# Attention feeding a two-layer MLP: transposing the first units on TensorE, attending them a step sooner, and summing half of the first large chunk's first layer ahead, pair by pair

## The chip, the cores and the metric

One NeuronCore of a Trainium2 chip runs the whole kernel as one launch. The engines are TensorE (PE; its weight loads are listed as PEld), VectorE (DVE), ScalarE (ACT), GpSimd (POOL) and SyncE (SP), which issues the DMAs here. Each engine works through its own list of instructions in order and waits at semaphores for the others. The metric is the device time of one execution in microseconds (us), given as the median of several runs.

## The reference

Eight batches of eight heads with 576 tokens and head width 64. Each row of scores keeps its 32 largest entries before the softmax; the heads' outputs are put side by side as 512 features of 4608 tokens, and a two-layer MLP with a leaky ReLU follows.

```python
scores = scale * np.matmul(q, k.transpose(0, 1, 3, 2))
kth = np.partition(scores, -top_k, axis=-1)[..., -top_k:-top_k + 1]   # top_k = 32
scores = np.where(scores >= kth, scores, -1000000000.0)
scores = scores - np.max(scores, axis=-1, keepdims=True)
attn = np.exp(scores)
attn = attn / (np.sum(attn, axis=-1, keepdims=True) + 1e-09)
attn_out = np.matmul(attn, v)
...
x = attn_out.transpose(0, 2, 1, 3).reshape(B * S, H * D)   # 4608 x 512
h = x @ w_in                                               # 512 x 2048
g = np.maximum(0.01 * h, h)
return g @ w_out                                           # 2048 x 512
```

## The kernel before

**Units.** The attention is cut into 144 units. A whole unit is 128 queries of one pair of heads, and works on 128 x 2 x 576 scores. As 576 is four and a half times 128, the last (or, in odd batches, first) 64 queries of two pairs share a unit. A batch has 18 units: in even batches four query tiles, each over the four pairs (whole), and then two shared ones. So units 0 to 3 are the first 128 queries of batch 0 for pairs 0 to 3, units 4 to 7 the next 128, and so on up to 15; units 16 and 17 are the shared ones.

**Steps.** A loop over s writes the order of every engine's list by hand (the scheduler is told to leave it alone). At step s VectorE picks the 32 largest of unit s (`top_k`, L250 to L258, in four rounds, `slot()`); POOL masks unit s-1 (L268, L269), ScalarE takes its exponents (L272) and their sum (`ze`, L277); and unit s-2 is divided by that sum: reciprocal on VectorE (`rz`, L281), two multiplications on ScalarE (L284), together `weights_of`. Then unit s-2 is transposed. In the usual way (`transpose`) ScalarE splits the words into halves (two copies, L293), SyncE writes them to memory (L294) and reads them back by a DMA transpose (L298) into `wT`, of which there are three buffers. For the units in `HASTY` TensorE transposes instead (nine instructions, L308, into the PSUM buffers called `wide`), and ScalarE copies the result to `wT` (`keep_transposed`, L314).

Where `weights_of` stands in a step depends on the unit: usually after the first round of picks; in steps below `HURRY` (20) after the second (`late`), unless s-1 or s-2 is in `HURRIED`; and before the first round if s-2 is in `HURRIED` (`at_first`, again below step 20). In a list worked in order, an earlier place of the reciprocal also makes VectorE wait earlier for the sum.

**Values.** Two units at a time are multiplied with v on TensorE (L335, into a `wide` buffer) and copied by ScalarE (L349) into `x`, the MLP's input. `values_at` says at which step this stands, and whether in its middle or at its end: for units below 14, four steps after the pair, MIDDLE; after that three steps, END; and one step less for the pairs in `HURRIED` (15, 23, 31).

**Scores.** At the end of each even step the scores of units s+2 and s+3 are computed (L220): each unit takes a `wide` buffer (two of them, two banks each), and both share the one `narrow` buffer (two banks). ScalarE copies them out (L227). Units 0 and 1 go through `first_scores` instead (L236), which takes two `wide` buffers a unit and no `narrow`.

**MLP.** The tokens are cut into chunks, two of 128 and then 17 of 256. A chunk may start when all of its units have their values (`ready_at`, `attended`): chunk 0 after units 0 to 3, chunk 1 after 4 to 7, chunk 2 after 8 to 15. `mlp(ch)` is a generator. For the small chunks (`EARLY`) the first layer is `hidden_of_few` (L359), with Prelu on ScalarE (L364), transposes (L375) and their copies (L376). For the large ones it is 64 matmuls (L391), four (one for each pair's 128 features, `c`) for each of 16 blocks `f` of the hidden width; two blocks share a PSUM bank `ph`, and ScalarE's Prelu reads both (L397) into `gT`. The second layer is 16 matmuls for each 128 tokens (L403, bank `pz`), a copy to `o_sb` (L412) and the store (L413). `ph`, `pt` and `pz` share a pool of two banks.

Seven times a step `mlp_steps(budget)` lets the generator issue some matmuls: until chunk 2 is ready 500 columns' worth, then the backlog spread evenly to the step at which the next chunk is ready. So the place of every matmul in TensorE's list is fixed when the program is built.

Of the kernel before, what the change touches and what calls it, by code (L numbers as in the profile page):

```python
# [9 lines left out]
F32 = mybir.dt.float32  # L10
# [10 lines left out]
def kernel(  # L21
# [13 lines left out]
    nc = tc.nc  # L35
    NPAIR, P, S = qT.shape
# [8 lines left out]
    HP = DMODEL // P  # L45
    B = NPAIR // HP
    HS = S // 2
    NARROW = 224
    WIDE = S - NARROW
    NFC = DFF // P  # L50
    WCH = 1024
    LEFT = S % P
    assert D == 64 and S == 576 and HP == 4 and B % 2 == 0 and LEFT == 64
    CHUNKS = [128] * 2 + [256] * 17
    assert sum(CHUNKS) == B * S
    CHMAX = max(CHUNKS)
# [23 lines left out]
    w_in = [const.tile([P, DFF], F32, name=f"w_in{c}") for c in range(HP)]  # L80
# [113 lines left out]
    units = []  # L194
    for b in range(B):
        first = b % 2 == 1
        whole = [Unit(b, [b * HP + hp], q0 + LEFT * first)
                 for q0 in range(0, S - LEFT, P) for hp in range(HP)]
        left = [Unit(b, [b * HP + hp, b * HP + hp + 1], 0 if first else S - LEFT)
                for hp in range(0, HP, 2)]  # L200
        units += left + whole if first else whole + left

    def scores(us):


        narrow = ps_sc.tile([P, 2, 512], F32, name="narrow")
        ps = {}
        for k, u in enumerate(us):
            wide = ps_sc.tile([P, 2, 512], F32, name="wide", bufs=2)
            ps[u] = ((wide[:, :, 0:WIDE], 0, WIDE),  # L210
                     (narrow[:, :, k * NARROW:(k + 1) * NARROW], WIDE, S))

        order = ((us[0], 0), (us[0], 1), (us[1], 1), (us[1], 0))
        for u, part in order:
            to, k0, k1 = ps[u][part]
            for n in range(0, len(u.parts), 2):
                for i, pi, side, r0 in u.parts[n:n + 2]:
                    qt, kt = qk_of[pi]
                    d = slice(side * D, (side + 1) * D)
                    nc.tensor.matmul(to[r0:r0 + u.rows, i, :], qt[d, u.q0:u.q0 + u.rows],  # L220
                                     kt[d, k0:k1], start=True, stop=True)
        for u in us:
            u.both = work.tile([P, 2, S], F32, name="s_sb", bufs=5)
            u.s = [u.both[:, i, :] for i in range(2)]
        for u, part in order:
            to, k0, k1 = ps[u][part]
            nc.scalar.copy(u.both[:, :, k0:k1], to)  # L227

    def first_scores(u):

        ps = [ps_sc.tile([P, 2, 512], F32, name="wide", bufs=2) for i in range(2)]
        for half in range(2):
            for i, pi, side, r0 in u.parts:
                qt, kt = qk_of[pi]
                d = slice(side * D, (side + 1) * D)
                nc.tensor.matmul(ps[i][:, half, 0:HS], qt[d, u.q0:u.q0 + P],  # L236
                                 kt[d, half * HS:(half + 1) * HS], start=True, stop=True)
        u.both = work.tile([P, 2, S], F32, name="s_sb", bufs=5)
        u.s = [u.both[:, i, :] for i in range(2)]
        for i in range(2):  # L240
            nc.scalar.copy(u.s[i].rearrange("p (h n) -> p h n", h=2), ps[i][:, :, 0:HS])
# [76 lines left out]
    x_of = {}  # L318
# [53 lines left out]
    def turned(j, g_of):  # L372
# [3 lines left out]
        nc.scalar.copy(gT[:, 4 * j:4 * (j + 1), 0:P], pt)  # L376
        yield 2 * P

    def mlp(ch):

        n = CHUNKS[ch]
        t0 = sum(CHUNKS[:ch])
        x = x_of[ch]
        if ch < EARLY:
            yield from hidden_of_few(ch, x)
        for f0 in range(0, NFC if ch >= EARLY else 0, 2):
            ph = ps_ml.tile([P, 2, CHMAX], F32, name="ph", tag="ml")
            for i in range(2):
                f = f0 + i
                for c in range(HP):  # L390
                    nc.tensor.matmul(  # L391
                        ph[:, i, 0:n], w_in[c][:, f * P:(f + 1) * P], x[c][:, 0:n],
                        start=(c == 0), stop=(c == HP - 1),
                    )
                    if c == 1 or i == 0 and c == HP - 1:
                        yield 2 * max(n, 225)
            nc.scalar.activation(gT[:, f0:f0 + 2, 0:n], ph[:, :, 0:n], AF.Prelu, alpha=SLOPE)  # L397
            yield 2 * max(n, 225)
        for r0 in range(0, n, P):
            m = min(P, n - r0)  # L400
            pz = ps_ml.tile([P, 512], F32, name="pz", tag="ml")
            for f in range(NFC):
                nc.tensor.matmul(  # L403
                    pz[0:m, 0:DMODEL], gT[:, f, r0:r0 + m], w_out[f // 4][:, f % 4, :],
                    start=(f == 0), stop=(f == NFC - 1),
                )
                if f % 2 and f + 1 < NFC:
                    yield 2 * DMODEL
                if f == 7 and ch in few:
                    yield from turned(NFC // 4 - 1, few[ch])  # L410
            o_sb = work.tile([P, DMODEL], F32, name="o_sb", bufs=1)
            nc.scalar.copy(o_sb[0:m], pz[0:m, 0:DMODEL])  # L412
            nc.sync.dma_start(out[t0 + r0:t0 + r0 + m, :], o_sb[0:m])  # L413
            yield 2 * DMODEL

    def mlp_cost(ch):
        n = CHUNKS[ch]
        if ch < EARLY:
            return NFC * DMODEL + NFC // 4 * (HP * 512 + 2 * P)
        return NFC * HP * max(n, 225) + -(-n // P) * NFC * DMODEL  # L420
# [4 lines left out]
    def mlp_steps(budget):  # L425
        owed[0] += budget
        while owed[0] > 0:
            if running[0] is None:
                if not ready:
                    owed[0] = 0.0  # L430
                    return
                running[0] = mlp(ready.pop(0))
            cost = next(running[0], None)
            if cost is None:
                running[0] = None
            else:
                owed[0] -= cost
                backlog[0] -= cost
# [2 lines left out]

    LAG = 3
    HURRY = 20
    HURRIED = (15, 23, 31)
    HASTY = (14, 15, 23, 31)
    UNHURRIED = 14
    MIDDLE, END = 0, 1

    def values_at(n):

        if n < UNHURRIED:
            return (n | 1) + LAG + 1, MIDDLE
        return (n | 1) + LAG - ((n | 1) in HURRIED), END

    steps = units

# [11 lines left out]
    def attended(*place):  # L468
        for at, ch in ready_at:
            if at == place:  # L470
                ready.append(ch)
                backlog[0] += mlp_cost(ch)

    def slot_budget(s):

# [9 lines left out]
    with tc.manual_schedule():  # L485
# [52 lines left out]
        for s in range(len(steps) + LAG + 1):  # L538
            cur, old, older, new = unit(s), unit(s - 1), unit(s - 2), ()
            if s % 2 == 0:  # L540
                new = [u for u in steps[s + 2:s + 4] if u]
            picks = top_k(cur) if cur else iter(())
            budget = slot_budget(s)

            def slot():
                next(picks, None)

            at_first = s < HURRY and s - 2 in HURRIED
            if at_first:
                weights_of(older)  # L550
            slot()
            if old:
                mask(old, 0)
                mask(old, 1)
            late = s < HURRY and not {s - 1, s - 2} & set(HURRIED)
            if older and not late and not at_first:
                weights_of(older)
            mlp_steps(budget)
            weighed = values(s, MIDDLE)
            at_once = s - 2 in HURRIED or any(at == (s, MIDDLE) for at, _ in ready_at)  # L560
            if at_once:
                keep(weighed, s, MIDDLE)
            slot()
            if older and late:
                weights_of(older)
            if s - 2 in HASTY:
                transpose_in_haste(older)
            mlp_steps(budget)
            if old:
                exponents(old, 0)  # L570
            mlp_steps(budget)
            if older:
                keep_transposed(older) if s - 2 in HASTY else transpose(older, lambda: mlp_steps(budget))
            if not older or s - 2 in HASTY:
                mlp_steps(budget)
            slot()
            slot()
            mlp_steps(budget)
            if old:
                exponents(old, 1)  # L580
                sums(old)
            mlp_steps(budget)
            if not at_once:
                keep(weighed, s, MIDDLE)
            if new and s < HURRY:
                scores(new)
            keep(values(s, END), s, END)
            if new and s >= HURRY:
                scores(new)
            budget = slot_budget(s + 1)  # L590
            mlp_steps(budget)
            load_more(s)
# [59 lines left out]
```

## Time and profile before

| what | value |
|---|---|
| median of 8 runs | 1472.07 us (1469.79 to 1473.73) |
| profiled execution | 1473.73 us, its span 1471.8 us |
| TensorE busy | 1394.5 us (95%), mean granted clock 0.981 |
| VectorE busy | 1322.1 us (90%) |
| ScalarE, POOL busy | 1097.9 us (75%), 1096.4 us (74%) |
| first-layer matmuls of chunk 0 start | 134.03 us |
| values of units 14 and 15 end, chunk 2 starts | 228.7 us |
| VectorE's period from step 16 on | 207.72, 216.80, 225.56, 234.36 us |

A busy share is an average over stages: the first 64 us load and round the weights, from 66 us on the steps run, and after about 1385 us only the MLP of the last chunks is left. Times in the trace are counted from the start of the span. An f32 matmul of 256 or 512 columns appears as two records (x32 is 16 matmuls); a transpose of 128 columns as one. In a row of the timeline, the number in brackets is the engine's idle time before it, and the arrow names what ended it.

### The profile page before, as it was taken

How to read it: one execution, taken by the hardware profiler on the slowest of the kernel's cores; microseconds unless marked ns; L12 is line 12 of the kernel's file. 1: busy time of each engine (PE TensorE's matmuls, PEld its weight loads, DVE VectorE, ACT ScalarE, POOL GpSimd, SP SyncE). 2: the span in 40 equal slices, each digit the busy share in tenths (PEclk: the TensorE clock that was granted, in tenths of full speed). 3: DMA queues.
4: the chain of work that ended last, by engine and by line, in shares of the span. 5: the costliest groups of instructions: out<-in, count | busy, mean ns of one | idle time of the engine just before them, and what ended most of it. 6: DMA issues, size and time to landing. Idle time of an engine off the chain costs nothing.

```text
span 1471.8 us, 24096 instructions
## 1 busy us (share of the span) xinstructions
PE 1394.5 (95%) x8068; PEld 927.8 (63%) x8068; DVE 1322.1 (90%) x3400; ACT 1097.9 (75%) x1979; POOL 1096.4 (74%) x743
## 2 busy tenths in 40 slices
PE   6716999999999999999999999999999999999999
PEld 2304548676766666767666666666666666666674
DVE  7899999999999999999999999999999999999600
ACT  8657878777887777777777777777777777777710
POOL 3188888878788888888888787878787878787700
PEclk9957999999999999999999999999999999999999
DMA  9724543655367455665557544765467544654510
GB/s 332 298 67 135 145 113 100 178 152 149 92 185 203 137 137 154 167 180 145 145 158 191 151 137 122 186 186 150 123 165 208 137 136 131 169 135 138 143 50 14
DMA packets 388795, 222.29 MB, mean 151 GB/s; under 512 B 333888, under 2 KB 333888, under 8 KB 386624
## 3 DMA queue, kind: packets, MB, share of 16 engines
q1 hardware_dynamic: 388672, 220.77, 53.8%
q8 instruction: 63, 1.03, 0.3%
q14 instruction: 60, 0.49, 0.1%
HBM read 46.14 MB, written 92.01 MB: 94 GB/s over the span
## 4 chain that ended last, share of the span: by engine, by line
PE 80%; DVE 13%; DMA 3%; ACT 2%; issue 1%; SPq 0%; DVEq 0%; ACTq 0%
PE pz L403 31%; PE ph L391 30%; PE wide L335 10%; DVE tops L255 6%; PE wide L220 6%; DVE pairs L258 4%; PE narrow L220 3%; DMA raw<-in_weights_dram 2%; DVE pairs L250 1%; DMA wT<-apart 1%; ACT wT L127 0%; DVE w_out L155 0%; DMA apart<-split 0%; ACT split L293 0%; PE wide L308 0%
## 5 line engine op out<-in xcount | busy, mean ns | idle before, releaser
L268 POOL TENSOR_SCALAR pen<-s_sb,tops 128x576 f32<-128x576 f32 x288 | 637.5, 2213 | 210.6 <-DVE tops L255 142.7
L255 DVE MAX8 tops<-pairs 128x8 f32<-128x288 f32 (+1 forms) x1152 | 635.9, 591 | 0.0
L403 PE MATMUL pz<-w_out,gT 128*128 128x512 f32 x1152 | 505.3, 595 | 2.4 <-ACT scale L364 2.4
L391 PE MATMUL ph<-x,w_in 128*128 128x256 f32 x2176 | 482.6, 381 | 0.0
L258 DVE MATCH_REPLACE8 pairs<-tops,pairs 128x288 f32<-128x288 f32 (+1 forms) x864 | 460.1, 538 | 0.0
L391 PEld LDWEIGHTS ph<-x,w_in 128*128 128x128 f32 x2176 | 409.5, 190 | 76.4 <-issue 22.2
L269 POOL TENSOR_TENSOR s_sb<-s_sb,pen 128x576 f32<-128x576 f32 x288 | 406.6, 1412 | 24.1
L403 PEld LDWEIGHTS pz<-w_out,gT 128*128 128x128 f32 x1152 | 216.4, 190 | 267.2 <-issue 262.5
L293 ACT COPY split<-s_sb 128x1152 uint16<-128x1152 uint16 x280 | 309.4, 1146 | 0.0
L284 ACT ACTIVATE s_sb<-s_sb,rz 128x576 f32<-128x576 f32 x288 | 207.6, 773 | 41.5 <-DVE rz L281 41.4
L272 ACT ACTIVATE s_sb<-s_sb,nbias 128x576 f32<-128x576 f32 x288 | 222.3, 772 | 13.3 <-POOL s_sb L269 13.3
L250 DVE TENSOR_TENSOR pairs<-s_sb 128x576 f32<-128x576 f32 x288 | 213.3, 779 | 9.9
L335 PEld LDWEIGHTS wide<-wT,vt 128*64 128x64 f32 x3200 | 161.7, 139 | 68.3 <-issue 35.5
L335 PE MATMUL wide<-wT,vt 128*64 128x128 f32 (+1 forms) x3200 | 179.2, 268 | 25.9 <-ACT s_sb L227 21.8
L227 ACT COPY s_sb<-wide 128x704 f32<-128x704 f32 x142 | 107.2, 755 | 21.8 <-PE wide L220 21.8
L397 ACT ACTIVATE gT<-ph 128x512 f32<-128x512 f32 x136 | 80.6, 593 | 56.4 <-PE ph L391 55.7
L349 ACT COPY x<-wide 128x128 f32<-128x128 f32 (+1 forms) x160 | 32.2, 260 | 114.5 <-PE wide L335 114.5
L220 PE MATMUL wide<-kt,qt 64*128 64x352 f32 (+1 forms) x392 | 75.5, 499 | 26.6 <-ACT s_sb L227 23.5
L412 ACT COPY o_sb<-pz 128x512 f32<-128x512 f32 x36 | 21.0, 585 | 98.6 <-PE pz L403 98.5
L227 ACT COPY s_sb<-narrow 128x448 f32<-128x448 f32 x142 | 68.7, 536 | 1.1 <-PE narrow L220 0.4
L281 DVE RECIPROCAL rz<-ze 128x2 f32<-128x2 f32 x144 | 22.3, 155 | 47.5 <-ACT ze L277 47.4
L258 DVE MATCH_VALUE_LOAD pairs<-tops,pairs 128x8 f32 x864 | 62.5, 72 | 0.0
(63 smaller groups left out, 622.1 us busy)
## 6 DMA issues: line engine op xcount, KB each, us to landing
apart<-split SPq DMA_DIRECT2D x280, 288.0 KB, 2.1
raw<-in_weights_dram SPq DMA_DIRECT2D x16, 1024.0 KB, 7.4
vt<-in_vk_dram SPq DMA_DIRECT2D x32, 320.0 KB, 3.6
out_dram<-o_sb SPq DMA_DIRECT2D x36, 256.0 KB, 2.6
qt<-in_qT_dram SPq DMA_DIRECT2D x20, 288.0 KB, 3.2
kt<-in_kT_dram SPq DMA_DIRECT2D x20, 288.0 KB, 3.7
raw<-in_qT_dram SPq DMA_DIRECT2D x12, 288.0 KB, 3.4
raw<-in_kT_dram SPq DMA_DIRECT2D x12, 288.0 KB, 3.7
```

The costliest lines, as they stand in the source:

```text
L220: nc.tensor.matmul(to[r0:r0 + u.rows, i, :], qt[d, u.q0:u.q0 + u.rows], kt[d, k0:k1], start=True, stop=True)
L250: nc.vector.tensor_tensor(pairs[:, :, n, :], u.both[:, :, 0:HS], u.both[:, :, HS:S], op)
L255: nc.vector.max(out=u.tops[:, i, r, :], in_=rest[i])
L258: nc.vector.match_replace(out=rest[i], in_to_replace=u.tops[:, i, r, :], in_values=rest[i], imm_value=LOWEST)
L268: nc.gpsimd.tensor_scalar(pen, u.s[i], u.tops[:, i, ROUNDS - 1, 7:8], MASKED, ALU.is_lt, ALU.mult)
L269: nc.gpsimd.tensor_tensor(u.s[i], u.s[i], pen, ALU.add)
L272: nc.scalar.activation(u.s[i], u.s[i], AF.Exp, bias=u.nbias[:, i:i + 1], scale=SCALE, accum_out=u.z[:, i:i + 1])
L284: nc.scalar.activation(u.s[i], u.s[i], AF.Copy, bias=0.0, scale=u.rz[:, i:i + 1])
L293: nc.scalar.copy(split, pairs[:, :, h])
L335: nc.tensor.matmul(po[side * D:(side + 1) * D, o, :], vt[:, c, side, :], u.wT[:, c + side * NKC if c + 1 < NKC else c, r:r + n], start=(c ...
L391: nc.tensor.matmul(ph[:, i, 0:n], w_in[c][:, f * P:(f + 1) * P], x[c][:, 0:n], start=(c == 0), stop=(c == HP - 1),)
L403: nc.tensor.matmul(pz[0:m, 0:DMODEL], gT[:, f, r0:r0 + m], w_out[f // 4][:, f % 4, :], start=(f == 0), stop=(f == NFC - 1),)
```

## The change

Five edits, which build on each other:

1. `HASTY` gains units 0, 1, 2, 3 and 7: these are transposed on TensorE.
2. `HURRIED` gains 3 and 7, and `values_at` applies it below 14 too: the values of units 2 and 3 move from the middle of step 7 to the end of step 5, those of units 6 and 7 from the middle of step 11 to the end of step 9. Through `late` and `at_first`, the reciprocals of units 2 and 6 move from after the second round of picks to after the first, those of units 3 and 7 to before the first.
3. In batch 0 the last two query tiles are taken pair by pair: units 8 and 9 are both tiles of pair 0, units 10 and 11 of pair 1, and so on. So chunk 2 gets the features of one pair after the other.
4. `begin_hidden` sums the first eight of chunk 2's 16 blocks over pairs 0 and 1 (16 matmuls, from the middle of step 15 on) and pair 2 (eight matmuls, from the middle of step 17 on), each when its values are there. The blocks lie in four banks: the two of `narrow` and both of the pool that `ph` and `pz` use. `mlp(2)` then adds pair 3 (eight matmuls) before Prelu, and goes on with the other eight blocks as before.
5. As `narrow` is taken, step 16 computes the scores of units 18 and 19 with `first_scores`, one unit after the other; its matmul takes the rows of shared units.

```diff
+        tiles = [(0,), (P,), (2 * P, 3 * P)] if b == 0 else [(q0,) for q0 in range(0, S - LEFT, P)]
         whole = [Unit(b, [b * HP + hp], q0 + LEFT * first)
-                 for q0 in range(0, S - LEFT, P) for hp in range(HP)]
+                 for q0s in tiles for hp in range(HP) for q0 in q0s]
...
-                nc.tensor.matmul(ps[i][:, half, 0:HS], qt[d, u.q0:u.q0 + P],
+                nc.tensor.matmul(ps[i][r0:r0 + u.rows, half, 0:HS], qt[d, u.q0:u.q0 + u.rows],
                                  kt[d, half * HS:(half + 1) * HS], start=True, stop=True)
...
+    begun = {}
+
+    def begin_hidden(ch, pairs):
+        n = CHUNKS[ch]
+        x = x_of[ch]
+        if ch not in begun:
+            first = ps_sc.tile([P, 2, 512], F32, name="narrow").rearrange("p h (f n) -> p h f n", n=CHMAX)
+            begun[ch] = [first[:, 0], first[:, 1]]
+            begun[ch] += [ps_ml.tile([P, 2, CHMAX], F32, name="ph", tag="ml") for k in range(2)]
+        done = 0
+        for f in range(NFC // 2):
+            for c in pairs:
+                nc.tensor.matmul(begun[ch][f // 2][:, f % 2, 0:n], w_in[c][:, f * P:(f + 1) * P], x[c][:, 0:n],
+                                 start=(c == 0 and f % 2 == 0), stop=False)
+                done += 1
+                if done % 2 == 0:
+                    yield 2 * n
...
-            ph = ps_ml.tile([P, 2, CHMAX], F32, name="ph", tag="ml")
+            first = 0
+            if ch in begun and f0 < NFC // 2:
+                ph, first = begun[ch][f0 // 2], HP - 1
+            else:
+                ph = ps_ml.tile([P, 2, CHMAX], F32, name="ph", tag="ml")
             for i in range(2):
                 f = f0 + i
-                for c in range(HP):
+                for c in range(first, HP):
                     nc.tensor.matmul(
                         ph[:, i, 0:n], w_in[c][:, f * P:(f + 1) * P], x[c][:, 0:n],
-                        start=(c == 0), stop=(c == HP - 1),
+                        start=(c == 0), stop=(c == HP - 1 and (i == 1 or not first)),
                     )
-                    if c == 1 or i == 0 and c == HP - 1:
+                    if not first and (c == 1 or i == 0 and c == HP - 1):
                         yield 2 * max(n, 225)
...
-                running[0] = mlp(ready.pop(0))
+                running[0] = ready.pop(0)
...
-    HURRIED = (15, 23, 31)
-    HASTY = (14, 15, 23, 31)
+    HURRIED = (3, 7, 15, 23, 31)
+    HASTY = (0, 1, 2, 3, 7, 14, 15, 23, 31)
...
     def values_at(n):
-        if n < UNHURRIED:
-            return (n | 1) + LAG + 1, MIDDLE
-        return (n | 1) + LAG - ((n | 1) in HURRIED), END
+        if (n | 1) in HURRIED:
+            return (n | 1) + LAG - 1, END
+        return ((n | 1) + LAG + 1, MIDDLE) if n < UNHURRIED else ((n | 1) + LAG, END)
...
             if at == place:
-                ready.append(ch)
+                ready.append(mlp(ch))
                 backlog[0] += mlp_cost(ch)
+        for last, pairs in ((11, (0, 1)), (13, (2,))):
+            if values_at(last) == place:
+                ready.append(begin_hidden(EARLY, pairs))
...
             if new and s < HURRY:
-                scores(new)
+                if s == 16:
+                    first_scores(new[0])
+                    first_scores(new[1])
+                else:
+                    scores(new)
```

## The prediction

> **What bounds the kernel now.** I read the chain of waits first, then the busy time by stretches, then the TensorE, SyncE and VectorE rows around the first chunks. The chain by engine:
>
> ```profile
> PE 80%; DVE 13%; DMA 3%; ACT 2%; issue 1%; SPq 0%; DVEq 0%; ACTq 0%
> ```
>
> TensorE's 80% are the later part, VectorE's 13% (191 us) the first. The stretches (us; then busy us of PE, PEld, DVE, ACT, POOL; the last three columns are granted clock, DMA share, GB/s):
>
> ```profile
> 75.00:100.00 25.00, 4.21 (x16) 2.50 (x16) 24.86 (x67) 12.18 (x23) 21.64 (x15) 0.52 0.17 48
> 100.00:125.00 25.00, 7.04 (x56) 5.58 (x56) 24.76 (x66) 16.68 (x31) 21.19 (x14) 0.64 0.50 135
> 125.00:150.00 25.00, 19.99 (x94) 11.58 (x96) 24.83 (x67) 21.12 (x41) 20.92 (x15) 0.82 0.44 127
> 400.00:1400.00 1000.00, 997.06 (x5962) 681.16 (x5959) 946.18 (x2465) 788.95 (x1448) 807.90 (x539) 1.00 0.58 156
> ```
>
> VectorE is full from the start; TensorE idles for 39 of 50 us up to 125 and then never: what it does earlier is gain only if nothing it needs later is late. Where the chain passes from VectorE to TensorE for the last long time:
>
> ```profile
> 439.29 0.08 DVE rz L281
> ...
> 443.72 4.05 DMA apart<-split
> ...
> 447.82 4.71 DMA wT<-apart
> ...
> 452.57 1.31 PE wide L335 x20
> ```
>
> So up to 452 TensorE has no reserve against transposed probabilities. The weighted values (L335) and the transposes (L308) in between:
>
> ```profile
> 226.36 2.40 PE L335 MATMUL wide<-wT,vt 128*64 128x128 f32 x40 [1.06 <-ACT wT L314]
> 251.95 2.55 PE L335 MATMUL wide<-wT,vt 128*64 128x64 f32 x80
> 270.55 2.55 PE L335 MATMUL wide<-wT,vt 128*64 128x64 f32 x80
> 289.10 2.40 PE L335 MATMUL wide<-wT,vt 128*64 128x128 f32 x40
> 295.44 1.43 PE L308 MATMUL wide<-ident,s_sb 128*128 128x128 f32 x9
> ```
>
> They are values(14,15), (16,17), (18,19), (20,21) and the transposes of unit 23. The DMA transposes that feed the middle three:
>
> ```profile
> 247.33 2.69 SPq L298 DMA_TRANSPOSE wT<-apart  x1
> 265.19 2.49 SPq L298 DMA_TRANSPOSE wT<-apart  x1
> 282.73 2.61 SPq L298 DMA_TRANSPOSE wT<-apart  x1
> ```
>
> With 4.6 us from issue to landing (the median for L298) they land at 251.9, 269.8 and 287.3: 0.1, 0.8 and 1.8 us before their use. That is all the room a TensorE that arrives earlier has, unless these land earlier too. Last, VectorE's reciprocals of units 15 and 23:
>
> ```profile
> 216.72 0.17 DVE L281 RECIPROCAL rz<-ze 128x2 f32<-128x2 f32 x1 [0.24 <-ACT ze L277]
> 290.66 0.15 DVE L281 RECIPROCAL rz<-ze 128x2 f32<-128x2 f32 x1
> ```
>
> Up to 290.66 it waited 0.24 us in all, so the transposes of unit 23 can start at best after 290.83 plus the first L284 (0.76): 291.6, which is 3.9 before 295.56, where their work starts in the chain. Behind them the order of TensorE is the same in both kernels to the end.
>
> **The change, part by part.** Step s is unit s on VectorE; step 16 starts at 207.72, a step is 8.87 us, and the second slot's reciprocal comes 4.5 us into it, the first slot's 2.95.
>
> *Early transposes (units 0 to 3, 7).* Each drops two split copies (2.09 us on ScalarE), two DMA writes and a DMA transpose, whose issues nothing in SyncE's queue waits behind, and adds nine transposes (1.43 warm) and two copies (1.07, from L314). TensorE idles there, so its share costs nothing; if cold (the values at 112.03 took 4.54 us after 13.5 idle, 2.40 when warm) it is 2.7 each, still inside idle time. POOL's order is unchanged. Units 2, 3, 6 and 7 get their reciprocal earlier. For unit 3: its sum is ready at 109.5 (last exponent after POOL, 108.3; copies done 108.4; exponent and sum 1.1), wanted at 110.13: no stall. For unit 7, from unit 6's reciprocal at 139.8: two L284 1.34, Prelu 0.57, exponent 0.76, gT copy 0.57, two splits 2.09, exponent and sum 1.1 make 146.3 against 145.59 wanted: VectorE loses 0.8. Bounds: 0 (if the Prelu waits for nothing and the copies go faster) and 2.5 (TensorE one score group, 2.3, late); I take 0.8, which the rows give directly.
>
> *Chunk 0 sooner.* values(2,3) end near 120 instead of 134.1. Hence chunks 0 and 1 are done near 208.5 and TensorE waits 4 us before the transposes of unit 14, of which 1.7 are filled with the first four matmuls ahead. This pays nothing by itself: the next step is VectorE's.
>
> *Steps 16 to 18, worked with VectorE 0.8 late.* Reciprocal of unit 14 at 211.5, L284 to 213.0, transposes 212.5 to 213.8 (213.15 before). Then ten matmuls of the new sum, 0.438 each (14.01/32): 218.2. Scores (18,19) now take both wide banks per unit: 1.3 for unit 18, then two copies of 0.55 to 220.9, unit 19 to 222.1, its copies to 223.3 (222.8 before). Two more matmuls 0.9, values(12,13) 222.95 to 225.3, transposes of unit 15 to 226.5 (225.3 before), then eight matmuls of pair 2: 3.5. values(14,15) start at 230.05, not 226.36: **3.7 late, with 24 of 64 matmuls of chunk 2's first layer (10.5 us) done.**
>
> *Steps 18 and 19 on ScalarE.* Two x copies, then Prelu (0.57) as pair 3 comes in: two before L284(16), one on each side of the exponent: split(16) 238.5, sum of unit 17 at 241.6, wanted at 239.7, so VectorE loses 1.9. The score copies (2.24), Prelu, L284, exponent: split(17) at 246.5 against 242.95. Split to L298's issue was 4.4 (242.95 to 247.33), landing 4.6: 255.45. values(16,17) move from 252.0 to 255.45. Unit 18's sum costs VectorE 1.3 more; 4.0 late in all, below the 5.2 at which unit 23's reciprocal would decide (its L284 now comes at 296.0).
>
> *Steps 21 to 25.* Behind values(16,17) TensorE now has only chunk 2's second layer left (16 first-layer matmuls, 7.0, less than before), so it waits. After them: copies 0.8, scores copied 2.3, L284 1.34, exponent 0.76, split 2.1, 2.2 to the transpose, 4.6: values(18,19) at 272.05 (before 270.62). In the next round o_sb's copy now stands before split(21) and waits for four matmuls behind the scores (2.2 + 3.5 after 274.55): split(21) at 281.7 against 278.29, values(20,21) at 290.6 against 289.17. So **unit 23's transposes start 1.4 later than before.** Check of the sum: −10.5 ahead, +3.7 late, +0.85 for a bank that Prelu holds, and waits of 2.5, 1.5 and 3.4 before the three values: +1.4.
>
> *From there to the end* TensorE has no idle time to give (997.06 of 1000), so the 1.4 stays. In the profiled execution: 1473.73 (span 1471.8 and 1.9 around it) becomes 1475.1; against the median 1472.07, 1.66 below it, **1473.5**.
>
> Unknown prices. The three landings ran from 4.4 to 6.5 around 4.6: −0.2 each if quick, +1.9 for one slow one; I take the median. The matmuls ahead have the shape of L391's and its price. That unit 19's scores wait for unit 18's copies has no row of its own: 0 if the copies come while TensorE still writes, 2.4 if each of the two waits for both; I take 1.3, from the two copies of L241 (1.18) and their release.
>
> The row on the clock: 4.54 after 13.52 idle, but 0.86, full speed, at 120.58 after 2.38 idle; the 2.3 idle before unit 14's transposes is of the second kind. The Trainium skill ("TensorE: Matmul & The Clock Gate", Part 1) says that the clock halves after an idle window of about 3.4 us, free-running, and is released after as long of work. It speaks against transposes strewn over idle stretches, and by it, if the window fell badly, the ten matmuls would run at half speed for 3.4 us and add an estimated 1.7; by the rows, none.
>
> **The rivals.** *B, faster:* ScalarE gets through steps 18 and 19 with less waiting, and unit 23's reciprocal decides: 3.9 less 0.8 plus 0.24, −3.3: 1468.7. For it: VectorE's 0.24; against it: L298's landings. The whole 10.5 (1461.6) is excluded by that reciprocal. *C, slower:* ScalarE's queue in steps 17 to 19 holds longer than my sums: a Prelu or x copy stands behind TensorE's pair 2 and 3 matmuls and everything behind it waits, as o_sb's copy did for 3.08 at 219.76. It passes on one to one; it decides once values(14,15) start after 231.6. Priced at that 3.08 once more: 1476.6. *D, slower:* the early reciprocals hold VectorE 2.5 instead of 0.8: +1.7, 1475.2, and with one score group late in step 5 as well 1476.
>
> **How the numbers follow.** This kernel's runs tell 0.2% (2.9 us) from no change. Mine, within that: 0.48, own range 1470.5 to 1475. B 0.14, C 0.26, D 0.12, the last two counted as slower. The range leaves out the lower half of B and what lies above C by more than 1.3, two thirds of a slow landing's 1.9: 1469.0 to 1477.8.
>
> **What would show it.** Right: TensorE idle before all three of values(16,17), (18,19), (20,21) with the DMA transpose as releaser; values(14,15) near 230; reciprocals of units 7, 17, 18 waiting 0.8, 1.9, 1.3; after unit 23's transposes the same work in the same time. Wrong: values(16,17) before 253, or no wait of VectorE in steps 19 and 20 (then B); a granted clock under 0.9 between 205 and 230, or values(14,15) after 232 (then C).

## The result, and the profile after

The changed kernel takes **1477.64 us** (median of 11 runs, 1475.48 to 1480.32) against 1472.11 us for the kernel before on the same chip (32 runs): ratio 1.0035, 95% interval [1.0025, 1.0044], so 5 us slower. The profiled execution took 1478.69 us, its span 1476.8, against 1473.73 and 1471.8. The forecast was 1473.5 and, as the likeliest case, no change.

Of the 4.96 us between the two profiled executions 1.36 lie ahead of the first pick of unit 0, which VectorE starts at 67.42 instead of 66.06 us. A second profile of each kernel (below) has it at 64.77 and 66.15: the load stage varies from one execution to the next. So I count from the first pick from here on. First pick to end: 1405.7 and 1405.1 before, 1409.4 and 1410.5 after; **4.5 us are lost on the mean, and they are lost behind the first pick.**

First the chain of waits by engine, after:

```profile
PE 84%; DVE 6%; DMA 6%; ACT 3%; issue 1%; SPq 0%; POOL 0%; DVEq 0%; ACTq 0%; POOLq 0%
```

Before it was PE 80%, DVE 13%, DMA 3%. The first chunks' work does come sooner, and TensorE bounds earlier, but DMA has doubled. The busy time by stretches, after (us; busy PE, PEld, DVE, ACT, POOL; granted clock, DMA share, GB/s):

```profile
100.00:125.00 25.00, 17.75 (x130) 12.52 (x130) 24.79 (x67) 14.81 (x33) 20.98 (x15) 0.73 0.00 1
400.00:1400.00 1000.00, 996.95 (x5952) 681.75 (x5952) 950.65 (x2476) 790.13 (x1449) 811.33 (x542) 1.00 0.57 156
```

TensorE is busy for 17.75 of the 25 us from 100 on, where it was for 7.04, so idle time there was filled as the change says; and behind 400 it has as little to give as before (996.95 of 1000; before, 997.06). What was gained must be lost in between. TensorE's rows there, after (in brackets the idle time before a row, and what ended it):

```profile
214.22 1.56 PE L395 MATMUL narrow<-x,w_in 128*128 128x256 f32 x6 [2.62 <-ACT x L351]
215.61 1.15 PE L310 MATMUL wide<-ident,s_sb 128*128 128x128 f32 x9
...
232.60 2.40 PE L337 MATMUL wide<-wT,vt 128*64 128x128 f32 x40
...
258.92 1.39 PE L337 MATMUL wide<-wT,vt 128*64 128x64 f32 x40 [0.20 <-DMA wT<-apart]
...
274.57 0.80 PE L337 MATMUL wide<-wT,vt 128*64 128x64 f32 x20 [0.31 <-DMA wT<-apart]
...
293.15 1.31 PE L337 MATMUL wide<-wT,vt 128*64 128x128 f32 x20 [2.68 <-DMA wT<-apart]
...
300.04 1.20 PE L310 MATMUL wide<-ident,s_sb 128*128 128x128 f32 x9
```

These are the first matmuls ahead with the transposes of unit 14, values(14,15), the second halves of values(16,17), (18,19) and (20,21), and the transposes of unit 23, T(23). All three later values now end a wait for a DMA transpose, where before they came just behind its landing. T(23) starts 232.6 us after the first pick; before, 229.4 (295.44 less 66.06). VectorE's reciprocals that waited, after:

```profile
147.53 0.17 DVE L283 RECIPROCAL rz<-ze 128x2 f32<-128x2 f32 x1 [0.67 <-ACT ze L279]
170.39 0.17 DVE L283 RECIPROCAL rz<-ze 128x2 f32<-128x2 f32 x1 [0.56 <-ACT ze L279]
179.79 0.17 DVE L283 RECIPROCAL rz<-ze 128x2 f32<-128x2 f32 x1 [0.44 <-ACT ze L279]
245.30 0.17 DVE L283 RECIPROCAL rz<-ze 128x2 f32<-128x2 f32 x1 [3.23 <-ACT ze L279]
253.60 0.17 DVE L283 RECIPROCAL rz<-ze 128x2 f32<-128x2 f32 x1 [0.92 <-ACT ze L279]
```

They are units 7, 9, 10, 17 and 18, 5.82 us in all; before, VectorE lost 0.24 up to here.

### The profile page after: what moved, and what is told of

The parts are those of the page before. It is cut to its first block, busy times and chain, and to the rows that moved or that the text cites. A ratio compares the mean times of both kernels' runs of the same rounds, so it can differ in the third digit from the quotient of the medians.

```text
span 1476.8 us, 24168 instructions
## 1 busy us (share of the span) xinstructions
PE 1404.6 (95%) x8113; PEld 933.0 (63%) x8113; DVE 1322.2 (90%) x3400; ACT 1094.1 (74%) x1979; POOL 1096.4 (74%) x743
## 4 chain that ended last, share of the span: by engine, by line
PE 84%; DVE 6%; DMA 6%; ACT 3%; issue 1%; SPq 0%; POOL 0%; DVEq 0%; ACTq 0%; POOLq 0%
PE pz L429 33%; PE ph L417 29%; PE wide L337 11%; PE wide L222 6%; PE narrow L222 3%; DMA wT<-apart 2%; DVE tops L257 2%; DMA raw<-in_weights_dram 2%; DVE pairs L260 2%; ACT split L295 1%; DMA apart<-split 1%; DVE pairs L252 1%; PE ph L361 1%; ACT s_sb L274 0%; ACT s_sb L286 0%
## 5 line engine op out<-in xcount | busy, mean ns | idle before, releaser
L417 PE MATMUL ph<-x,w_in 128*128 128x256 f32 x2120 | 470.6, 381 | 0.8 <-ACT gT L423 0.8
L417 PEld LDWEIGHTS ph<-x,w_in 128*128 128x128 f32 x2120 | 398.8, 190 | 75.7 <-issue 22.1
L295 ACT COPY split<-s_sb 128x1152 uint16<-128x1152 uint16 x270 | 298.9, 1147 | 0.0
L337 PEld LDWEIGHTS wide<-wT,vt 128*64 128x64 f32 x3200 | 158.0, 137 | 50.4 <-issue 36.9
```

The costliest lines, as they stand in the source:

```text
L295: nc.scalar.copy(split, pairs[:, :, h])
L337: nc.tensor.matmul(po[side * D:(side + 1) * D, o, :], vt[:, c, side, :], u.wT[:, c + side * NKC if c + 1 < NKC else c, r:r + n], start=(c ...
L417: nc.tensor.matmul(ph[:, i, 0:n], w_in[c][:, f * P:(f + 1) * P], x[c][:, 0:n], start=(c == 0), stop=(c == HP - 1 and (i == 1 or not first)),)
```

## The experiments

Two theories stood at the start. Theory Q: the loss comes from steps 16 to 20, where the matmuls ahead stand before the values of units 14 and 15, the Prelus hold ScalarE's queue, VectorE waits for sums, and the DMA transposes land late. Rival E: the early reciprocals of edit 2 hold VectorE, and that passes to the end. All runs in one table: the median with that of the kernel before on the same chip, the ratio, T(23) counted from the first pick, the time from T(23) to the end, and what VectorE waited for the sums of units 17 and 18.

| kernel | median (before), us | ratio, 95% | T(23) | T(23) to end | units 17, 18 |
|---|---|---|---|---|---|
| before; again | 1472.11 | | 229.4; 229.4 | 1176.4; 1175.7 | none |
| changed | 1477.64 (1472.11) | 1.0035 [1.0025, 1.0044] | 232.6 | 1176.8 | 3.23, 0.92 |
| changed, again | 1477.54 (1472.84) | 1.0032 [1.002, 1.0044] | 233.1 | 1177.4 | 4.09, 0.92 |
| e1: edits 1, 2 | 1471.98 (1471.71) | 1.0005 [0.9996, 1.0014] | 228.8 | 1177.2 | none |
| e3: pairs 0, 1 | 1484.9 (1471.71) | 1.0091 [1.0077, 1.0104] | 233.4 | 1185.2 | 3.46, 0.98 |
| e4: hasty to 21 | 1480.8 (1471.71) | 1.0061 [1.0047, 1.0075] | 235.4 | 1175.2 | 5.20, 2.41 |
| e5: four blocks | 1471.07 (1471.71) | 0.9992 [0.9981, 1.0002] | 225.8 | 1177.3 | none |
| e6: none ahead | 1477.62 (1471.24) | 1.004 [1.0028, 1.0052] | 232.6 | 1176.1 | 0, 1.49 |
| e7: e5, new scores | 1471.31 (1471.24) | 1.0002 [0.9994, 1.0011] | 226.6 | 1176.6 | 0, 0.57 |
| e8: pairs 0, 1 | 1473.85 (1471.24) | 1.0014 [1.0005, 1.0022] | 229.9 | 1175.6 | 0.54, 0.92 |
| e9: e5, sooner | 1492.91 (1471.24) | 1.0137 [1.0118, 1.0157] | 229.4 | 1196.8 | none |
| e12: filled wait | 1476.57 (1472.84) | 1.0023 [1.0013, 1.0033] | 231.8 | 1176.6 | 4.10, 0.93 |
| e13: x at once | 1475.65 (1472.84) | 1.0025 [1.0016, 1.0034] | 232.7 | 1177.2 | 2.55, 0.91 |

Where the MLP's pacing is as before (all but e3 and e9), T(23) to the end is 1175.2 to 1177.4 in every profile: what a kernel gains or loses is decided by T(23).

**The early part alone** (edits 1 and 2; what it lacks of the changed kernel, shortened).

```diff
-    tiles = [(0,), (P,), (2 * P, 3 * P)] if b == 0 else [(q0,) for q0 in range(0, S - LEFT, P)]
...
-        for last, pairs in ((11, (0, 1)), (13, (2,))):
-            if values_at(last) == place:
-                ready.append(begin_hidden(EARLY, pairs))
...
-                if s == 16:
-                    first_scores(new[0])
-                    first_scores(new[1])
```

> Only edits 1 and 2: units 0 to 3 and 7 transposed on TensorE, their values a step sooner; no matmul ahead, old order of units, old scores in step 16. Theory Q (the loss comes from steps 16 to 20: the sums of pairs 2 and 3 stand in front of values and Prelus, ScalarE's queue and VectorE wait, the transposed probabilities land late): chunk 0 starts near 121, VectorE still loses 1 to 2 us in steps 8 to 12, but nothing in steps 19 and 20, and the time is that of before within 1.5 us: 1471 to 1473.5. Rival E (the early reciprocals' stalls pass to the end): 1474 to 1476.

Within the error of no change, and T(23) is 0.6 us earlier. VectorE's three early waits are there (0.67, 0.55, 0.44 for units 7, 9 and 10), and nothing of them arrives: up to T(23) the landings decide, not VectorE. Rival E falls.

**Only pairs 0 and 1 ahead**, pair 2 with pair 3 after the values.

```diff
-                ph, first = begun[ch][f0 // 2], HP - 1
+                ph, first = begun[ch][f0 // 2], HP - 2
...
-        for last, pairs in ((11, (0, 1)), (13, (2,))):
+        for last, pairs in ((11, (0, 1)),):
```

> The changed kernel with only pairs 0 and 1 summed ahead (16 matmuls of chunk 2, not 24); pairs 2 and 3 (16 matmuls) are added when all values are there. Theory Q with the Prelus as its main part: values of units 14 and 15 come 3.5 us earlier than in the changed kernel (near 229), but each Prelu now waits for four matmuls (1.75) instead of two, so split of unit 16 and the sum of unit 17 are no earlier, VectorE still loses 2 to 4 us in step 19, and the time is 1475 to 1478. If pair 2's eight matmuls ahead of the values are the main part: 1472.5 to 1474.5. Rival E: no change, 1477 to 1478.

This one can't be read as meant. Where a block begun ahead yields once for its four matmuls, only half their columns are taken off the backlog; the rest spoils the pacing of later chunks, and 8 to 9 us are lost behind T(23). It was made again with the columns counted:

```diff
-                    if not first and (c == 1 or i == 0 and c == HP - 1):
+                    if first < HP - 1 and (c == 1 or i == 0 and c == HP - 1):
```

> The changed kernel with only pairs 0 and 1 summed ahead (16 matmuls), pairs 2 and 3 after the values, and their columns counted in the backlog as issued (in e3_pairs01 half of pair 2 was not counted). If the eight matmuls of pair 2 before the values of units 14 and 15 are the loss: values(14,15) at 228 to 229.5 and 1471.5 to 1474. If Prelus that wait for pair 3 in ScalarE's queue are the loss: they now wait for two pairs instead of one, and it is 1476 to 1479, with VectorE's wait in step 19 still over 2 us.

Without pair 2's eight matmuls in front of them the loss falls from 0.35% to 0.14%, inside the first theory's time, and VectorE waits 0.54 for unit 17 where it waited 3.23. The other theory would have kept that wait over 2. The values of units 14 and 15 did not come at the 228 to 229.5 expected but at 230.90, 164.4 after the first pick; the changed kernel has 165.2 and, again, 166.7. TensorE ran at half clock for a while in this profile (see below), which ate part of the 3.5 us; and for 1.07 of it TensorE now waits for the copies of unit 15's transposes, a wait that pair 2's matmuls had filled.

**Units 16 to 21 on TensorE too**, so that no DMA transpose lands late.

```diff
-    HASTY = (0, 1, 2, 3, 7, 14, 15, 23, 31)
+    HASTY = (0, 1, 2, 3, 7, 14, 15, 16, 17, 18, 19, 20, 21, 23, 31)
```

> The changed kernel with units 16 to 21 also transposed on TensorE (nine transposes, 1.2, and two copies, 1.07, in place of split, store and DMA transpose: 2.1 + 2.2 + 4.6). Theory Q: TensorE no longer waits for landings before the values of units 16 to 21 and ScalarE's queue is 1.0 shorter in each of steps 18 to 23, so the matmuls ahead are worth something: 1469 to 1473.5; the transposes of unit 23 then start within 1 us of VectorE's reciprocal of unit 23. Rival E: the loss stays, 1476.5 or more (six more transposes of 1.2).

A miss. The transposes of unit 16 now stand in TensorE's list, and wait for ScalarE:

```profile
233.27 1.13 PE L417 MATMUL narrow<-x,w_in 128*128 128x256 f32 x4 [0.69 <-ACT gT L423]
235.75 2.11 PE L310 MATMUL wide<-ident,s_sb 128*128 128x128 f32 x9 [1.35 <-ACT s_sb L286]
237.66 5.38 PE L417 MATMUL ph<-x,w_in 128*128 128x256 f32 x20
```

The matmuls behind them feed Prelus that stand ahead of the next exponents, so the sum of unit 17 is 5.20 us late, and VectorE loses 9.97 us up to unit 23. Taking the landings away in this way lengthens the waits in ScalarE's list; what they cost by themselves it doesn't show.

**Four blocks ahead instead of eight** (12 matmuls, in the pool's two banks; `narrow` stays free, so step 16 computes its scores as before).

```diff
-            first = ps_sc.tile([P, 2, 512], F32, name="narrow").rearrange("p h (f n) -> p h f n", n=CHMAX)
-            begun[ch] = [first[:, 0], first[:, 1]]
-            begun[ch] += [ps_ml.tile([P, 2, CHMAX], F32, name="ph", tag="ml") for k in range(2)]
+            begun[ch] = [ps_ml.tile([P, 2, CHMAX], F32, name="ph", tag="ml") for k in range(2)]
...
-        for f in range(NFC // 2):
+        for f in range(NFC // 4):
...
```

> The changed kernel with four blocks instead of eight summed ahead (12 matmuls, 5.3 us), in the two banks of the MLP's pool only; narrow stays free, and step 16 computes scores as before. Theory Q: before the values of units 14 and 15 stand four matmuls less (1.75), the second unit's scores no longer wait for the first unit's copies (1.3) and two Prelus leave ScalarE's queue: values of 14 and 15 near 228.5, VectorE's loss in step 19 under 1.5, time 1472 to 1475. Rival E: as the changed kernel or worse, 1477 or more.

T(23) comes 3.6 us earlier than before the change, and now it waits for its own reciprocal:

```profile
222.88 2.40 PE L337 MATMUL wide<-wT,vt 128*64 128x128 f32 x40
...
250.63 1.39 PE L337 MATMUL wide<-wT,vt 128*64 128x64 f32 x40 [1.12 <-DMA wT<-apart]
...
292.06 1.44 PE L310 MATMUL wide<-ident,s_sb 128*128 128x128 f32 x9 [1.24 <-ACT s_sb L286]
```

That is the forecast's case B, with VectorE deciding. Both the place and the time are better than expected for this run (values(14,15) near 228.5, 1472 to 1475). First pick to end is 1403.2, 2.2 less than the mean of the two profiles before; the medians show 0.6, which the interval can't tell from nothing. So half the blocks turn the loss into no loss, but into no gain that was measured. The same with the changed kernel's scores in step 16:

```diff
+                if s == 16:
+                    first_scores(new[0])
+                    first_scores(new[1])
```

> Four blocks (12 matmuls) ahead in the pool's two banks, as in e5_four_blocks, but with step 16's scores by first_scores as in the changed kernel. What differs from e5_four_blocks (1471.1) is the price of the two-bank scores by itself. My step of 1.3 us for them: values(14,15) at 224 to 225 instead of 222.9, and 1471 to 1472.5 in all. If each of the two scores waits for both copies (2.4 us) and the loss passes on: 1473.5 to 1475. If it is all hidden: 1470.5 to 1471.5.

The values of units 14 and 15 come 160.6 after the first pick instead of 156.6, of which 1.7 is a late start of the scores (half clock again) and 2.3 the scores themselves: 9.6 us from the first score to those values instead of 7.3. The time, 1.0002 against 0.9992, is not told apart, and 1471.31 lies in the first and the third of the ranges expected.

This run differs from the changed kernel in one thing: it lacks the second four blocks (12 more matmuls ahead, in `narrow`). With them the ratio is 1.0035 [1.0025, 1.0044], without them 1.0002 [0.9994, 1.0011]. **So those blocks cost the 5 us.** Leaving out only pair 2 (e8) brings back 3.1 of them.

**No matmuls ahead**, everything else as in the changed kernel.

```diff
-        for last, pairs in ((11, (0, 1)), (13, (2,))):
+        for last, pairs in ():
```

> The changed kernel without the matmuls ahead (edit 4 left out): early transposes, the pair-by-pair order and the two-bank scores of units 18 and 19 in step 16 stay; all 64 first-layer matmuls of chunk 2 come after the values of units 14 and 15, as before the change. Theory Q (the loss comes from the matmuls ahead standing before the values and from Prelu holding ScalarE's queue): 1471 to 1473.5, VectorE waits under 1 us for a sum in step 19. Theory T (the two-bank scores of step 16 are the cause): near the changed kernel, 1475.5 to 1478, with values(14,15) 3 us or more later than in the kernel with edits 1 and 2 alone (224.7).

This went against Theory Q as I had put it, and Theory T's time held: with nothing ahead the kernel is as slow as with 24 matmuls. TensorE's rows, e6:

```profile
212.53 2.18 PE L310 MATMUL wide<-ident,s_sb 128*128 128x128 f32 x9 [3.73 <-ACT s_sb L286]
...
218.69 2.73 PE L238 MATMUL wide<-raw 64*64 64x288 f32 x16 [0.73 <-ACT s_sb L243]
222.16 4.30 PE L337 MATMUL wide<-wT,vt 128*64 128x128 f32 x40 [0.73 <-ACT s_sb L243]
```

After 3.73 us of idling TensorE works at half clock until 226: the transposes take 2.18 (1.15 in the changed kernel), unit 19's scores 2.73 (1.74), values(12,13) 4.30 (2.40). The granted clock says so:

```profile
215.00:220.00 5.00, 3.67 (x25) 2.17 (x29) 5.00 (x13) 2.86 (x7) 3.58 (x4) 0.50 0.37 84
220.00:225.00 5.00, 4.27 (x39) 3.10 (x35) 5.00 (x16) 2.52 (x4) 4.42 (x4) 0.50 0.00 0
```

The stretches are read as above: 0.50 is half clock for ten microseconds. So values(14,15) start 163.5 after the first pick, 3.2 later than before the change, and with no head start behind them T(23) is 3.2 later too. The kernel with edits 1 and 2 alone has the same 3.73 us of idling and a clock of 0.50 from 215 to 220, and its values start at 159.4: there unit 18's and 19's scores share `narrow` and need not wait for one another. So the two theories were no alternatives: step 16's two-bank scores cost what Theory T says when TensorE comes to them cold, and the matmuls ahead cost their own time but keep it warmer.

**The backlog sooner**, on e5.

```diff
-        return backlog[0] / ((until + 1 - s) * SLOTS)
+        return backlog[0] / max((until + 1 - s) * SLOTS - 5, 1)
```

> e5_four_blocks with the backlog spread over five slots fewer, so that the MLP's matmuls due before the next chunk stand ahead of the last transposes and values instead of between and behind them. Theory: in e5_four_blocks the head start is given back in waits of TensorE before values(16,17), (18,19) and (20,21); more work issued sooner does not help there and only delays the scores: 1471 to 1473. Rival: TensorE has work left over behind the transposes of unit 23 that could fill the waits: 1467.5 to 1470.

Worse than both theories had it, and elsewhere: T(23) is where it was before the change. TensorE's waits from 300 to 1400 us in e9 (total us, times, longest):

```profile
PE wide L337 <- DMA wT<-apart: 8.0, 13, 2.1
PE wide L337 <- DMA vt<-in_vk_dram: 3.4, 2, 2.9
PE wide L222 <- ACT x L351: 2.7, 7, 0.6
PE wide L337 <- ACT wT L316: 2.3, 1, 2.3
```

Before the change the same stretch has 3.0 us of waits (2.2 for `wT`, 0.8 for `vt`). Matmuls handed out sooner leave none for the waits that come later, here in all the chunks, so this says nothing on the head start.

**Both kernels profiled once more.**

> The kernel before, profiled a second time, to see how much of the 4.96 us between the two profiled executions is chance. If the start of VectorE's picks (66.06 us in the first profile) is an accident of each load: it moves by 0.5 us or more, and first pick to end stays within 0.7 us of 1405.7. If the first profile was a slow one behind the start: first pick to end 1404 to 1405.

> The changed kernel, profiled and timed again. Theory: the start at 67.42 us is chance (now 65 to 66.5), what is lost behind it is not: first pick to end 1408.5 to 1411, VectorE's wait in step 19 again 3 us or more, TensorE at half clock again after its wait in front of unit 21's values. Rival: the changed kernel starts later for a reason of its own: 67 or more again. Time 1476 to 1479 by both.

The kernel before repeats itself (first pick 66.15, so 0.09 later and not 0.5 or more; first pick to end 1405.1). The changed one starts at 64.77, so the late start was chance, and the loss behind it is 1410.5 less 1405.1. But TensorE ran otherwise than in its first profile: here it lost its clock at 211, and not at 292:

```profile
211.45 2.41 PE L395 MATMUL narrow<-x,w_in 128*128 128x256 f32 x6 [2.62 <-ACT x L351]
213.65 2.02 PE L310 MATMUL wide<-ident,s_sb 128*128 128x128 f32 x9
...
292.14 1.31 PE L337 MATMUL wide<-wT,vt 128*64 128x128 f32 x20 [2.82 <-DMA wT<-apart]
293.38 0.86 PE L222 MATMUL wide<-raw 64*128 64x352 f32 x4
294.07 0.92 PE L222 MATMUL narrow<-raw 64*128 64x224 f32 x8
```

The first profile has, behind idle times of the same 2.6 to 2.7 us, 1.56 and 1.15 for the first two rows (shown above), but for the scores behind values(20,21):

```profile
294.39 1.49 PE L222 MATMUL wide<-raw 64*128 64x352 f32 x4
295.66 1.71 PE L222 MATMUL narrow<-raw 64*128 64x224 f32 x8
```

From the first matmul behind the wait to the first score it is 8.47 us here and 6.79 there; from the first of those scores to the next matmul 3.82 there, and 2.14 before the change. Each is 1.7 us. VectorE lost 7.41 us in this execution up to unit 23, and T(23) waited 0.39 for its weights, so VectorE decided here as much as the landings.

**The last wait filled** with 14 spare transposes.

```diff
             for n, u in enumerate(due):
+                if u is steps[21]:
+                    for k in range(14):
+                        nc.tensor.transpose(po[:, n, :], ident, ident)
                 weigh_values(u, po[:, n, :])
```

> The changed kernel with 14 spare transposes of 128 columns (0.13 us each, 1.8 in all; their result is overwritten) in front of unit 21's values, where TensorE waited 2.68 us for the DMA transpose and then ran the next scores at a granted clock of 0.71, 1.7 us longer than before the change. Theory: the filled wait keeps the clock at 1.00, the transposes of unit 23 come 1.7 us sooner, and it takes 1475.5 to 1476.5. Rival: the clock falls there in few executions, or VectorE decides by then: 1477 to 1478.

The median lies just above the theory's 1476.5, and 1.0023 [1.0013, 1.0033] isn't told apart from 1.0032 [1.002, 1.0044]. In its profile the clock is 1.00 from 290 to 300, though 1.53 us of the wait are left; but it had already fallen at 209.63, and VectorE waited 4.10 for unit 17. Filling one wait closes one place of several.

**The values of units 10 and 11 to `x` at once.**

```diff
-            at_once = s - 2 in HURRIED or any(at == (s, MIDDLE) for at, _ in ready_at)
+            at_once = s == 15 or s - 2 in HURRIED or any(at == (s, MIDDLE) for at, _ in ready_at)
```

> The changed kernel with the copies of the values of units 10 and 11 to x (step 15) at once, where the changed kernel has them behind a copy to o_sb, two splits and an exponent, 6 us after the values. Theory: the 16 matmuls ahead then start 3 to 5 us sooner in TensorE's idle time, the transposes of unit 14 no longer stand behind them, the values of units 14 and 15 come 1.5 to 2.5 us sooner after the first pick (163 instead of 165.2), and it takes 1474 to 1476. Rival: ScalarE, which now waits for those values, passes the wait to VectorE: 1477 to 1478.5.

The time is inside the first theory's, its ratio again not told apart from the changed kernel's. The 2.62 us of idling are gone, and the matmuls ahead run from 211.22 at 1.00. Yet the values of units 14 and 15 come at 164.5 and not 163: the transposes of unit 14 wait 1.15 for their weights, and values(12,13) 0.73 for a score's copy. VectorE's wait for unit 17 is 2.55.

Neither the matmuls ahead without the early transposes of edit 1 nor the pair-by-pair order (edit 3) by itself was tried; e5 has both and loses nothing that was measured.

## Why the prediction was wrong in its likeliest case, point by point

The range held the time, and the likeliest case did not: it put T(23) 1.4 us later, and it is 3.2 and 3.7. That 1477.64 lies inside the range, 0.16 us below its upper end, is luck: the clock's fall, which the forecast put at nothing, is in some executions and not in others. Its places, moved to a first pick at 66.06 (the changed kernel's first profile less 1.36, its second plus 1.29):

| | forecast | first profile | second |
|---|---|---|---|
| values(14,15) start | 230.05 | 231.24 | 232.80 |
| first split of unit 17 | 246.5 | 248.50 | 250.07 |
| unit 17's values (landed) | 255.45 | 257.56 | 259.17 |
| unit 19's | 272.05 | 273.21 | 274.69 |
| unit 21's | 290.6 | 291.79 | 293.43 |
| T(23) | 296.84 | 298.68 | 299.18 |
| VectorE's waits up to unit 23 | 4.0 | 5.82 | 7.41 |

- **"This pays nothing by itself", the early transposes: right.** e1 is at 1.0005. Unit 7's wait was 0.67, forecast 0.8. The price of case D, which let the reciprocals' stalls pass on, falls with it.
- **"TensorE waits 4 us ... of which 1.7 are filled with the first four matmuls ahead": wrong.** One matmul ran before the wait. The other three need the values of units 10 and 11 in `x`, whose copy began at 213.75 in the profile, behind a copy to `o_sb` that waited 1.38 for TensorE: the values stand in the middle of step 15, but this copy, and with it the start of the sum, at the step's end, and not from the middle on as the change was described. The transposes of unit 14 stand behind these three matmuls and begin, moved as in the table, at 214.25 instead of 212.5. From this 1.75 come the 1.2 by which values(14,15) are late in the first profile; in the second the clock adds 1.56.
- **The two-bank scores, 1.3: about right.** From the first score to values(12,13), less the two matmuls (0.9) between, it is 3.8 in the changed kernel and 2.1 in e5: 1.7. With nothing to issue in between it is 2.3 (e7 against e5).
- **The eight matmuls of pair 2, 3.5: right, and the part that mattered most.** Leaving them out brings 1.0035 to 1.0014 (e8), 3.1 us at 1472.
- **"split(17) at 246.5": 2.0 too soon.** 1.2 came with the values; the other 0.8 is in ScalarE's list, over the two banks of `narrow`: the matmuls of the second bank wait for the Prelu that reads the first (0.69, at 237.36), and the next Prelu waits for them:

```profile
235.05 0.43 ACT L351 COPY x<-wide 128x128 f32<-128x128 f32 x2 [3.66 <-PE wide L337]
236.71 0.60 ACT L423 ACTIVATE gT<-narrow 128x512 f32<-128x512 f32 x1 [1.22 <-PE narrow L417]
238.52 0.60 ACT L423 ACTIVATE gT<-narrow 128x512 f32<-128x512 f32 x1 [1.22 <-PE narrow L417]
239.02 1.43 ACT L286 ACTIVATE s_sb<-s_sb,rz 128x576 f32<-128x576 f32 x2
```

  These are ScalarE's rows of the changed kernel from the values of units 14 and 15 to the weights of unit 16: 3.97 us. In e7, which takes no `narrow`, the same way is 3.01 (228.86 to 231.87), the second Prelu waiting 0.27.
- **VectorE's 4.0 "below the 5.2 at which unit 23's reciprocal would decide": the size failed.** Unit 17's 1.9 became 3.23 and 4.09, by the two terms above, and 1.0 (0.85 in the second profile) fell in steps 11 and 12, which I had at nothing; the second profile has another 0.88 for unit 15. Of the twelve profiles with edit 1, those eight have the waits of steps 11 and 12 in which the clock fell near 142 us (last section). With 5.82 and 7.41 both limits lie close together; the second profile's 0.39 of T(23) waiting for its weights shows VectorE's.
- **"By the rows, none" for the clock: wrong.** The estimate of 1.7, worked out from the Trainium skill ("TensorE: Matmul & The Clock Gate", Part 1), was the measured price, and one row of full speed after 2.38 us of idling was too little to say that it wouldn't fall due. The profile before had rows that say the opposite, and the forecast passed over them:

  ```profile
  197.43 2.62 PE L403 MATMUL pz<-w_out,gT 128*128 128x512 f32 x4 [2.14 <-ACT scale L364]
  199.98 1.45 PE L220 MATMUL wide<-kt,qt 64*64 64x352 f32 x8
  ```

  Behind 2.14 us of idling the four records take 2.62 where the same four take 1.98 at 203.08, the scores 1.45 where the changed kernel's take 0.82 (at 201.12), and the granted clock is 0.86 and 0.80 in the stretches from 195 to 200 and to 205. In the first profile it fell due in front of T(23). There it is partly repaid: unit 20's half of values(20,21) is done before the wait, 1.1 us that the forecast had behind it. So 1.2 + 1.7 − 1.1 make the 1.8 by which T(23) missed.
- **"TensorE has no idle time to give" behind T(23): right**, to the scatter of 1175.2 to 1177.4.
- **The signs named:** all of "right" came (a wait for the DMA transpose before each of the three values, 0.20, 0.31 and 2.68; the same time behind T(23)), but for the sizes. Of "wrong", neither sign of case C is in the first profile. In the second both are: a clock of 0.70 from 210 to 215, and values(14,15) at 232.80.
- **Case C came nearest** (1476.6; "decides once values(14,15) start after 231.6"): 231.24 and 232.80 stand on both sides of its point, and its place, ScalarE's queue in steps 17 to 19, is where the time went. Case B needs less ahead than the change has: e5 is it.

So the 10.5 us of matmuls done ahead are given back three times: as the delay of the values behind them, in ScalarE's list behind the Prelus that follow, and in TensorE's idle waits for the DMA transposes that this list makes late, with the clock's 1.7 on top where it falls. In the first profile values(14,15) come 4.9 us later after the first pick than before the change; from them to T(23) TensorE waits 2.0 for ScalarE and 3.6 for DMAs; with the clock's 1.7 that is 12.2 of the 13.7 to be explained (10.5 and the 3.2 of T(23)). The other 1.5 are not followed up. Why e5's and e7's profiles are 2 us shorter than those before from the first pick on, and their medians hardly, stays open; the load stage's part in the timed executions isn't seen.

## What to carry to other kernels

Work pulled into an engine's idle time is free only if it is done when the next urgent thing is due: count what of it can really start then (whose copy, in whose queue), and put no more ahead than fits; here, with the same scores in step 16, 12 matmuls cost nothing that was measured, 24 cost 5 us, and none at all cost 6, where those scores met a low clock. A head start is worth only what the next limit leaves: follow it to the first wait that doesn't move, here a DMA transpose whose input goes through ScalarE's list, before counting it. Before an idle time of some 2 us is called harmless, look at several executions: the clock's fall behind it is a matter of chance, and belongs in the range.

## What was not expected of the hardware

The clock fell after idle times of TensorE well under 3.4 us, in some executions and not in others. Those near 142 and 212 us can be compared over the runs. Behind 2.39 to 2.40 us of idling near 142 us, the second layer's first eight records took 5.19 to 5.40 us in eight profiles and 3.70 in four (e4, e5, e7, e12). TensorE's row in the changed kernel:

```profile
143.21 5.40 PE L429 MATMUL pz<-w_out,gT 128*128 128x512 f32 x8 [2.39 <-ACT scale L366]
```

And in e5, which has the same instructions up to there:

```profile
142.03 3.70 PE L427 MATMUL pz<-w_out,gT 128*128 128x512 f32 x8 [2.40 <-ACT scale L366]
```

The four are exactly those in which VectorE's waits for units 9 and 10 (0.34 to 0.56 and 0.44) are absent. Behind the 2.62 us near 212 the first three matmuls took 1.56 us in four profiles and 1.96 to 2.48 in five; behind 3.73 us it fell both times. The Trainium skill ("TensorE: Matmul & The Clock Gate", Part 1) has the fall after an idle window of about 3.4 us that runs freely. That chance has a part in it agrees with these rows; that so much idling is needed does not: 2.4 us were enough in eight profiles of twelve, 2.14 in both profiles of the kernel before (above), and in e4 1.35, behind 0.53 and 0.69 just ahead of it (nine transposes in 2.11, shown above; clock 0.66 from 235 to 240). Behind 1.49 to 1.50 us near 177 it fell in none of the twelve. Nor is the price always 1.7: in e6, where TensorE went on waiting, the clock was 0.50 for ten microseconds.
